# One of the last weight transfers of an attention and spectral-mixing kernel, issued as 16 pieces of 8 partitions

## The chip, the cores and the metric

The kernel runs on one core of a Trainium2 chip. The metric is the device time of one execution in microseconds (us). A run's time is a little longer than the span of its profile, which runs from the first to the last recorded instruction.

## The reference

The input is q, k and v of 8 batches, 8 heads, 576 positions and 64 channels, two stacks of 64 weight matrices of 512x512 (w_r and w_i), and one 512x512 matrix w_ch, all fp32. A sliding-window causal attention (window 64) comes first; its output, 8 x 576 x 512, goes through a mixing in the frequency domain.

```
scores = where(0 <= pos_q - pos_k < 64, q k^T / 8, -1e9)
x = softmax(scores) v                     # as [8, 576, 512]
X = rfft(x, axis=1)                       # the first 64 modes are kept
Yr = Xr w_r - Xi w_i                      # one 512x512 matrix per mode
Yi = Xr w_i + Xi w_r
y = irfft(Y, n=576)
u = x + y
out = u + max(u w_ch, 0)
```

The two weight stacks hold 2 x 64 x 512 x 512 x 4 B = 134 MB, and each weight is used once.

## The kernel before

**Stages.** Attention comes first, batch by batch, with the forward transform done as matmuls against tables of sines and cosines (`trigF`). Then, for each group of four modes, matmuls at line 175 multiply the transformed rows (`XQ`) by the weights. A tail transforms back, multiplies by `w_ch` and writes the output. Work is issued in the order in which it is written (a manual schedule); each engine has its own queue and works it off in order.

**The weights.** `wlist` is the order in which weights are loaded: 32 steps (a group of four modes and one half `hb` of the 512 input channels), each with w_r and then w_i (`ri` = 0 and 1), each of these as two loads of two modes. Two of these loads (of steps 3 and 31) are cut into two loads of one mode, so there are 130 loads, counted here from 0 by `nload`. A load reads fp32 from DRAM and writes bf16 to SBUF into a tile of 128 partitions x 2 modes x 2 rows x 512; 512 KB are written. All loads are issued on the queue of POOL (GpSimd), at line 156. The last group in this order is 13: step 30 is its first half, step 31 its second.

**Where loads go.** Two rings of tiles, `ringA` with 7 and `ringB` with 10, and some lent places hold the weights. From step 20 on (load 81 and later) only `ringA` is used. `load_weights` issues the next load when the ring's oldest tile is in `spent`, which `mode_half` fills after its matmuls are written down. So a load late in the kernel waits, on POOL, for the matmuls that used the load seven places ahead of it.

**The last nine loads** are 121 and 122 (w_r of step 30), 123 and 124 (w_i of step 30), 125 and 126 (w_r of step 31), 127 (w_i of step 31, two modes), and 128 and 129 (one mode each, 256 KB). `mode_half` for step 30 with `ri` = 0 uses loads 121 and 122, and its matmuls come on PE before those of all later loads. Between the calls of `mode_half`, `advance` puts other work on PE (lines 591 and 660).

**After the last load** PE multiplies, turns and transforms back; POOL has no DMA left and adds two tensors at line 731 in some of the output tiles. SP issues most of the output.

Of the kernel before, what the change touches and what calls it, by code (L numbers as in the profile page):

```python
# [17 lines left out]
NRA = 7  # L18
NRB = 10
WARM = 8  # L20
NEG = -1.0e30
MAGIC = 12582912.0
PSAFE = 3.14159
# [3 lines left out]
def kernel(  # L27
# [10 lines left out]
    nc = tc.nc  # L38
# [10 lines left out]
    HALF = DM // 2  # L49
    NJ = 2  # L50
# [51 lines left out]
    wlist = []  # L102
# [27 lines left out]
    nload = 0  # L130
# [5 lines left out]
    def load_weights(n):  # L136
        nonlocal nload
        while n > 0 and nload < len(wlist):
            at, ps, hb, ri = wlist[nload]
            if nload in lent:  # L140
                w = lent[nload]
            else:
                open_to = "a" if at >= 2 * EARLY else "aby" if at < EARLY + 2 else "ab"
                h = min(open_to, key=lambda h: held[h][0] if len(held[h]) == room[h] else -1)
                if len(held[h]) == room[h]:
                    if held[h][0] not in spent:
                        return
                    held[h].pop(0)
                held[h].append(nload)
                if h == "y":  # L150
                    w = lentY[0]
                    lentY.append(lentY.pop(0))
                else:
                    w = {"a": ringA, "b": ringB}[h].tile([128, 2, NJ, DM], BF16, name="wi" if ri else "wr", tag="wt")
            src = moe_w_i if ri else moe_w_r
            nc.gpsimd.dma_start(  # L156
                out=w[:, 0:len(ps)], in_=src[ps[0]:ps[-1] + 1, HALF * hb:HALF * hb + HALF, :].rearrange("g (p j) e -> p g j e", j=NJ))
            for i, p in enumerate(ps):
                wtiles[p, hb, ri] = w[:, i]
            nload += 1  # L160
            n -= len(ps)
# [26 lines left out]
    with tc.manual_schedule():  # L188
# [165 lines left out]
        warm = ps_m.tile([128, DM], FP32, name="warm", tag="misc")  # L354
        for _ in range(WARM):
            nc.tensor.matmul(out=warm, lhsT=idle[:, 0:128], rhs=idle, start=True, stop=True)
# [7 lines left out]
        at = scratch[:, 3 * NTF * NM:3 * NTF * NM + NTF]  # L364
# [8 lines left out]
        for nm in ("k", "q", "v"):  # L373
            load(1, nm)
        LEAD = 4
        load_weights(LEAD)
        nc.gpsimd.iota(Kb, pattern=[[64, NBLK]], base=0, channel_multiplier=0,
                       allow_small_or_imprecise_dtypes=True)
# [25 lines left out]
        prvm, curm = mask_t[:, 0, 0, 0:64], mask_t[:, 0, 0, 64:128]  # L404
        ve.tensor_scalar(out=curm, in0=Kf, scalar1=Mcol, scalar2=NEG, op0=ALU.is_gt, op1=ALU.mult)
        ve.tensor_scalar(out=prvm, in0=Kf, scalar1=Mcol, scalar2=NEG, op0=ALU.is_le, op1=ALU.mult)
        ve.tensor_copy(out=mask_t[:, 0, 1, :], in_=mask_t[:, 0, 0, :])
        ve.tensor_copy(out=mask_t[:, 0, 2:4, :], in_=mask_t[:, 0, 0:2, :])
        ve.tensor_copy(out=mask_t[:, 1], in_=mask_t[:, 0])
        ve.memset(mask_t[:, 1, 0:4:2, 0:64], NEG)  # L410

# [40 lines left out]
        def early_step(it):  # L452
            nonlocal step
            grp = step
            psm = ps_m.tile([128, DM], FP32, name="psm", tag="misc")
            for ri in range(2):
                mode_half(psm, grp, 0, ri, True, True)
                load_weights(due(it) - loaded())
            nc.scalar.copy(out=Yacc[grp], in_=psm)
            step += 1  # L460
# [4 lines left out]
        for it in range(-3, NU + 3):  # L465
# [23 lines left out]
            g = starts.get(it + 2)  # L489
# [3 lines left out]
            g = starts.get(it + 1)  # L493
            if g is not None and g + 2 < NG:
                load(g + 2, "v")
            if it >= 0:
                for f in trig[0:2]:
                    f()
                del trig[0:2]
            load_weights(due(it) - loaded())  # L500
        do_dft(NG - 1)
        while step < EARLY:
# [183 lines left out]
        pu, us, ps = {}, {}, {}  # L686
# [184 lines left out]
```

## Time and profile before

| | us |
|---|---|
| median of 3 runs | 441.37 (441.29 to 441.67) |
| the profiled execution | 441.02 |
| its span | 439.2 |
| PE busy | 350.0 (80%) |
| DVE busy | 219.9 (50%) |
| ACT busy | 173.7 (40%) |
| POOL busy | 143.4 (33%) |
| packets of the queue that POOL issues, share of 16 DMA engines | 98.6% |

A line of a timeline gives start, duration, engine, line, operation, out<-in and count; in square brackets stands the idle time of the engine just before it and what ended it. A line of the chain of waits gives start, duration and what the time went to. POOL's `DMA_DIRECT2D` is the issue of a transfer; the transfer lands later, and the profile gives the time from issue to landing by line. 15.9 us is the median for the w_i loads.

### The profile page before, as it was taken

What the parts mean: (1) busy time and instruction counts of PE and PEld (TensorE: products, weight loads), DVE (VectorE), ACT (ScalarE), POOL (GpSimd) and SP (SyncE); (2) the same over time, 40 slices, a digit from 0 to 9 for tenths busy, and PEclk for the clock granted to TensorE, in tenths of its full rate; (3) what the DMA queues carried; (4) which work ended last, traced back from release to release, by engine and by line L of the source; (5) the groups of instructions that cost most, each with busy time, mean ns of one, the idle gap of its engine ahead of it and who ended that gap; (6) DMA issues with size and microseconds to landing.
All of it is one profiled execution on the core that took longest, in us unless ns stands there. A gap on an engine that the chain in (4) does not pass through costs nothing.

```text
span 439.2 us, 10995 instructions
## 1 busy us (share of the span) xinstructions
PE 350.0 (80%) x4728; PEld 219.5 (50%) x4728; DVE 219.9 (50%) x447; ACT 173.7 (40%) x307; POOL 143.4 (33%) x211
## 2 busy tenths in 40 slices
PE   6999999998999997986336565766778766799994
PEld 3666767676767664662113223334454433453552
DVE  8588787876776763775014111212223122345773
ACT  5666667575667663533002101111122121124662
POOL 9333323323233233223232232122232222301773
PEclk9999999999999996988559556788889689899999
DMA  8999999999999999999999999999999999992887
GB/s 205 211 211 211 212 210 211 211 211 211 212 211 212 212 210 211 211 212 211 211 258 211 211 211 211 211 211 211 212 211 211 211 211 211 212 177 67 271 305 263
DMA packets 47873, 93.45 MB, mean 213 GB/s; under 512 B 3536, under 2 KB 3664, under 8 KB 47824
## 3 DMA queue, kind: packets, MB, share of 16 engines
q0 software_dynamic: 42000, 81.73, 98.6%
q1 hardware_dynamic: 5600, 10.62, 7.2%
q8 instruction: 37, 0.61, 0.5%
q10 hardware_dynamic: 224, 0.39, 0.3%
q14 instruction: 12, 0.10, 0.1%
HBM read 163.58 MB, written 9.44 MB: 394 GB/s over the span
## 4 chain that ended last, share of the span: by engine, by line
DMA 47%; PE 41%; issue 5%; ACT 3%; DVE 3%; POOL 1%; DVEq 0%; POOLq 0%
DMA wi<-in_moe_w_i_dram 24%; DMA wr<-in_moe_w_r_dram 11%; DMA rawk<-in_k_dram 7%; PE tr L222 6%; DMA wch<-in_moe_w_ch_dram 4%; PE s L269 4%; PE pt L289 4%; PE s L261 4%; PE s L281 3%; PE psm L175 3%; PE vb L234 3%; PE o L309 2%; PE psz L591 1%; PE psm L697 1%; PE pst L723 1%
## 5 line engine op out<-in xcount | busy, mean ns | idle before, releaser
L591 PE MATMUL psz<-wch,tr 128*128 128x512 f32 x176 | 67.2, 517 | 10.9 <-DMA wch<-in_moe_w_ch_dram 10.9
L156 POOL DMA_DIRECT2D wi<-in_moe_w_i_dram x62 | 43.9, 709 | 95.7 <-PE psm L175 49.2
L682 DVE CAST xw<-psz 128x512 fp32r<-128x512 f32 x36 | 24.9, 691 | 91.4 <-PE psz L591 90.9
L156 POOL DMA_DIRECT2D wr<-in_moe_w_r_dram x53 | 37.9, 714 | 87.9 <-PE psm L175 38.0
L175 PEld LDWEIGHTS <-XQ 128*32 128x32 bf16 x512 | 24.0, 165 | 81.0 <-issue 73.6
L273 DVE TENSOR_REDUCE mx<-s 128x4 fp32r<-128x512 f32 x72 | 49.5, 687 | 26.3 <-PE s L269 26.0
L568 ACT CAST tr<-ptx 128x512 fp32r<-128x512 bf16 x36 | 21.1, 587 | 103.8 <-PE ptx L584 103.8
L175 PE MATMUL psm<-wi,XQ 128*32 128x512 bf16 x244 | 34.0, 466 | 30.6 <-DMA wi<-in_moe_w_i_dram 30.6
L591 PEld LDWEIGHTS psz<-wch,tr 128*128 128x128 f32 x176 | 40.1, 252 | 17.4 <-issue 11.2
L175 PE MATMUL psm<-wr,XQ 128*32 128x512 bf16 x212 | 29.8, 485 | 22.0 <-DMA wr<-in_moe_w_r_dram 21.3
L283 ACT ACTIVATE p<-s 128x512 bf16<-128x512 f32 x72 | 39.8, 604 | 13.0 <-PE s L281 13.0
L226 ACT COPY kT<-tr 128x576 bf16<-128x576 bf16 x32 | 23.2, 724 | 24.4 <-PE tr L222 24.4
L731 POOL TENSOR_TENSOR ut<-ut,XQ 128x512 f32<-128x512 f32 x16 | 20.5, 1284 | 28.1 <-ACT XQ L730 27.5
L292 DVE COPY pts<-pt 128x1024 bf16<-128x1024 bf16 (+1 forms) x40 | 25.2, 629 | 8.3 <-PE pt L289 7.0
L269 PE MATMUL s<-kT,qT 64*64 64x128 bf16 (+1 forms) x576 | 29.2, 221 | 0.0
L261 PE MATMUL s<-mask_t,ident_bf 128*128 128x512 bf16 x72 | 28.4, 395 | 0.9 <-ACT p L283 0.8
L226 ACT COPY qT<-tr 128x576 bf16<-128x576 bf16 x32 | 23.3, 729 | 10.7 <-PE tr L222 10.7
L269 PEld LDWEIGHTS <-qT 64*64 64x64 bf16 x576 | 17.8, 107 | 18.0 <-issue 17.5
L281 PE MATMUL s<-mx,ident_r 128*128 128x512 f32 x72 | 26.4, 438 | 0.0
L289 PE MATMUL pt<-ident_bf,p 128*128 128x128 bf16 x288 | 23.8, 223 | 1.5 <-issue 1.3
L226 ACT COPY vT<-tr 128x576 bf16<-128x576 bf16 x32 | 23.3, 728 | 4.0 <-PE tr L222 3.9
L321 DVE TENSOR_TENSOR x_sb<-o,r 128x512 bf16<-128x512 f32 x32 | 22.1, 691 | 1.1
(182 smaller groups left out, 567.2 us busy)
## 6 DMA issues: line engine op xcount, KB each, us to landing
wi<-in_moe_w_i_dram POOLq DMA_DIRECT2D x60, 512.0 KB, 15.9
wr<-in_moe_w_r_dram POOLq DMA_DIRECT2D x53, 512.0 KB, 16.3
out_dram<-ut SPq DMA_DIRECT2D x31, 256.0 KB, 2.4
rawv<-in_v_dram POOLq DMA_DIRECT2D x16, 288.0 KB, 14.4
rawk<-in_k_dram POOLq DMA_DIRECT2D x15, 288.0 KB, 15.1
rawq<-in_q_dram POOLq DMA_DIRECT2D x15, 288.0 KB, 14.1
Ypair<-in_moe_w_r_dram POOLq DMA_DIRECT2D x5, 512.0 KB, 14.9
x_sb<-in_moe_w_r_dram POOLq DMA_DIRECT2D x4, 512.0 KB, 15.2
```

The source lines that it names most:

```text
L156: nc.gpsimd.dma_start(out=w[:, 0:len(ps)], in_=src[ps[0]:ps[-1] + 1, HALF * hb:HALF * hb + HALF, :].rearrange("g (p j) e -> p g j e", j=NJ))
L175: nc.tensor.matmul(out=psm[32 * g:32 * g + 32, :], lhsT=XQ[hb].rearrange("k s b m -> k (s b) m")[:, (3 * j + 1 - ri) * B:(3 * j + 5 - ri) ...
L222: nc.tensor.transpose(out=pt[ro, j, :], in_=raw[ro, TH * half + j, :], identity=ident_bf[ro, ro])
L226: nc.scalar.copy(out=to, in_=pt.rearrange("p j n -> p n j"))
L261: nc.tensor.matmul(out=s, lhsT=ident_bf, rhs=mask_t[:, mk], start=True, stop=True)
L269: nc.tensor.matmul(out=s[ro, t, lo:128], lhsT=lq, rhs=kT[ro, 64 * n - 64 + lo:64 * n + 64], start=False, stop=True, skip_group_check=True)
L273: nc.vector.tensor_reduce(out=mx, in_=s, axis=AX.X, op=ALU.max, negate=True)
L281: nc.tensor.matmul(out=s, lhsT=ident_r, rhs=mx.unsqueeze(2).to_broadcast([128, 4, 128]), start=False, stop=True, skip_group_check=True)
L283: nc.scalar.activation(out=p[:, 4 * c2:4 * c2 + 4, :], in_=s, func=ACT_F.Exp, scale=EX_SCALE)
L289: nc.tensor.transpose(out=pt[:, t, :], in_=st[u]["p"][:, t, :], identity=ident_bf)
L292: nc.vector.tensor_copy(out=ps[:, 0:nt, :], in_=pt[:, 0:nt, :])
L591: nc.tensor.matmul(out=pz, lhsT=tr[:, c, :], rhs=wch[:, c, :], start=(c == 0), stop=(c == NDCH - 1))
```

## The change

A load whose number is 9 before the end of the list (130 - 9 = 121, the first w_r load of step 30) is issued by a loop of 16 DMAs, each of 8 partitions, in place of one DMA of 128 partitions. The destination tile, the bytes and the place in the order are the same, and every other load goes through the same loop once.

```diff
+NSPLIT = 9
...
-            src = moe_w_i if ri else moe_w_r
-            nc.gpsimd.dma_start(
-                out=w[:, 0:len(ps)], in_=src[ps[0]:ps[-1] + 1, HALF * hb:HALF * hb + HALF, :].rearrange("g (p j) e -> p g j e", j=NJ))
+            src = (moe_w_i if ri else moe_w_r)[ps[0]:ps[-1] + 1, HALF * hb:HALF * hb + HALF, :]
+            src = src.rearrange("g (p j) e -> p g j e", j=NJ)
+            n8 = 8 if nload == len(wlist) - NSPLIT else 128
+            for at in range(0, 128, n8):
+                nc.gpsimd.dma_start(out=w[at:at + n8, 0:len(ps)], in_=src[at:at + n8])
```

## The prediction

> **What bounds the kernel now.** I read the page's DMA rows first, then POOL's timeline (early and late), then the end of the chain of waits, then PE's timeline around the load that is cut.
>
> ```profile
> GB/s 205 211 211 211 212 210 211 211 211 211 212 211 212 212 210 211 211 212 211 211 258 211 211 211 211 211 211 211 212 211 211 211 211 211 212 177 67 271 305 263
> ...
> q0 software_dynamic: 42000, 81.73, 98.6%
> ```
>
> The flow of weights is flat at 211 GB/s up to slice 35, and the DMA queue behind POOL is all of it. A load of 512 KB (524,288 B) takes 2.48 us at that rate. As long as something is queued this flow sets the time; a gap in it is lost.
>
> ```profile
> 9.50 0.74 POOL L156 DMA_DIRECT2D wi<-in_moe_w_i_dram  x1
> 10.23 0.57 POOL L209 DMA_DIRECT2D rawk<-in_k_dram  x1
> 10.78 0.56 POOL L209 DMA_DIRECT2D rawq<-in_q_dram  x1
> 11.32 0.73 POOL L156 DMA_DIRECT2D wi<-in_moe_w_i_dram  x1
> 12.49 0.55 POOL L209 DMA_DIRECT2D rawv<-in_v_dram  x1 [0.45 <-PE tr L222]
> 13.03 0.72 POOL L156 DMA_DIRECT2D wr<-in_moe_w_r_dram  x1
> 18.10 0.55 POOL L209 DMA_DIRECT2D rawk<-in_k_dram  x1 [4.35 <-DMA Ypair<-in_moe_w_r_dram]
> 18.64 0.55 POOL L209 DMA_DIRECT2D rawq<-in_q_dram  x1
> 20.68 0.71 POOL L156 DMA_DIRECT2D wr<-in_moe_w_r_dram  x1 [1.49 <-DMA wi<-in_moe_w_i_dram]
> 22.33 0.55 POOL L209 DMA_DIRECT2D rawv<-in_v_dram  x1 [0.95 <-PE vb L234]
> 23.51 0.70 POOL L156 DMA_DIRECT2D wi<-in_moe_w_i_dram  x1 [0.63 <-DMA rawq<-in_q_dram]
> ```
>
> This is the row that decides the case, and it lies far from the edit. The issue at 20.68 waited for the landing of a w_i load. Count back eight issues: the w_i load at 9.50. The issue at 23.51 waited for a rawq load; eight back stands rawq at 10.78. The trace's records of these issues name eight semaphores (104 to 111), taken in turn through all 177 issues of POOL. So an issue waits until the issue eight before it has landed: POOL has at most eight transfers under way, whatever their size.
>
> ```profile
> 363.04 0.71 POOL L156 DMA_DIRECT2D wi<-in_moe_w_i_dram  x1 [3.59 <-PE psm L175]
> 363.75 0.72 POOL L156 DMA_DIRECT2D wr<-in_moe_w_r_dram  x1
> 367.97 0.71 POOL L156 DMA_DIRECT2D wr<-in_moe_w_r_dram  x1 [3.50 <-PE psm L175]
> 368.68 0.72 POOL L156 DMA_DIRECT2D wi<-in_moe_w_i_dram  x1
> ...
> 382.94 1.10 POOL L156 DMA_DIRECT2D wi<-in_moe_w_i_dram  x2 [3.52 <-PE psm L175]
> ```
>
> These are loads 120, 121 (to be cut), 122, 123, and 128 with 129. Here PE's use of the tile seven loads back is what POOL waits for; the eighth transfer back has long landed. The two issues at 363 land after 14.1 and 15.9 us (minimum and maximum of their row), load 120 at 377.1 and load 121 at 379.6: some six loads lie in the queue.
>
> ```profile
> 377.93 14.12 DMA wr<-in_moe_w_r_dram
> 392.09 0.67 PE psm L175 x5
> ...
> 397.40 0.59 PE psm L175 x2
> ```
>
> ```profile
> 382.15 0.71 PE L175 MATMUL psm<-wr,XQ 128*32 128x512 bf16 x6 [2.03 <-DMA wr<-in_moe_w_r_dram]
> ```
>
> The chain goes from the issue of load 126 to its landing and into the last matmuls; PE resumes on load 122 at 382.15 after 2.03 us idle for it. The tail to the end hangs on these landings.
>
> **The change, step by step.** It removes one issue of 0.72 us on POOL and adds 16. The bytes stay.
>
> *Price of one piece.* No row has 16 rows of 2 KB (8 partitions x 2 modes). At line 156, 256 rows take 0.714 us and the 128 rows of loads 128 and 129 take 0.553 (0.548 and 0.558). That is 1.26 ns a row, so 16 rows come to 0.553 - 112 x 0.00126 = 0.41. Bounds: the shortest rows, 0.528 for 128 rows, give 0.37 by the same line, and I go down to 0.35; above, the full load's 0.71. I take 0.41.
>
> *Pieces 0 to 6* (16 pieces, from 0). Piece 0 waits for the transfer eight back, load 113, landed long ago; pieces 1 to 6 for loads 114 to 119. These land 2.48 us apart, so POOL now goes at the pace of landings. Their bytes (7/16 of 2.48 = 1.1 us) lie in the queue before load 120 has ended, and cost nothing.
>
> *Piece 7* waits for the transfer just ahead of the cut load, load 120: 377.1. In the early rows a freed issue starts 0.29 us after the last increment of the semaphore (landed 20.39, issued 20.68; 23.22 and 23.51). So piece 7 starts at 377.4, with only 1.1 us of bytes queued, half spent or more.
>
> *Pieces 7 to 15* follow one another: 9 x 0.41 = 3.7 us, to 381.1. Pieces 8 to 14 wait for pieces 0 to 6, landed by about 378.5; piece 15 waits for piece 7, issued 8 x 0.41 = 3.3 us before it, and isn't held if a piece lands within that time; by the price below it does (4.9 - 2.48, plus 0.16 of movement: 2.6). Queued behind all this on POOL are loads 122 to 129, and nothing else until 404.41 (line 731). Load 122 is thus issued at 381.1, not at 367.97.
>
> *Load 122 into an empty queue.* Every weight load of the trace finds a full queue, so I bound. Above: the first load of all, 288 KB, lands after 6.1 us; less 1.40 us of movement that leaves 4.7, in competition with SP's two loads of q and k. Below: SP's stores of 256 KB land after 2.4 us, of which 1.0 is movement at 263 GB/s: 1.4. With 2.48 of movement the load takes 3.9 to 7.2; I take 4.9, nearer to SP's rows, as theirs is the uncrowded queue, plus POOL's longer issue. It lands at 381.1 + 4.9 = 386.0; before, at 367.97 + 14.13 = 382.1. The loss is **3.9 us**. The Trainium skill ("DMA: Bandwidth & Descriptors", section "Anatomy of one DMA") puts the fixed part of a POOL transfer at about 2.0 us; with 2.48 of movement that would make 4.5, and the loss 3.5. No row here has it.
>
> *What passes on.* Loads 123 to 127 follow 0.71 us apart, faster than they move; their tiles are free by then (load 127 needs load 120's matmuls, done near 378). Loads 128 and 129 need the matmuls of 121 and 122, some two us after 386.0, with five loads or 12.4 us still queued. So the flow is whole again from 122 on, and every later landing is late by the same 3.9. On PE, from 382.15 to the wait at 392.09 there is hardly a gap, in an order that is fixed, so that nothing can be drawn forward into the longer wait. The first matmul on the cut load waits on up to eight semaphores for one; at 17 ns a semaphore row that is 0.14 us, under the wait for load 122, and would cost that 0.14 without it. A longer idle PE might also be clocked down: after the 2 us waits at 372.20 and 382.15 the four matmuls of line 591 took 2.06 us, later ones 1.17. They pay this already, so I add 0, at most 0.9.
>
> Sum: 441.02 of the profiled execution + 3.9 = 444.9; against the median, 441.37 + 3.9 = **445.3**.
>
> Ends: 0.35 a piece and 3.9 for load 122 give 377.4 + 3.15 + 3.9 = 384.45, +2.35. A piece at 0.71 alone gives +6.6; load 122 at 7.2 alone gives, with piece 15 then held by piece 7, about +7.8.
>
> **Rivals.**
>
> *Not held: no change.* If pieces don't wait eight back, POOL is busy 16 x 0.41 = 6.6 us from 363.75 to 370.4, and load 122 is issued 2.4 us late into a queue that lasts to 379.6; load 124 at 373.09 is on time again. 441.4. Against it: the early rows, where the waits stand.
>
> *The other side: trailing engines relieved.* A load's semaphore rises in 16 steps. For load 121 eight come from 374.0 to 376.1 and eight from 378.5 to 379.6; for load 129 from 391.5 to 393.5 and from 395.9 to 397.2. Eight engines trail and set each landing. If every piece's data went to the leading eight, these would end 2.48 later, at 396.0, and the trailing eight 2.48 sooner: 1.2 us gained, 440.2. It decides only if piece 7 isn't held, since held, the trailing engines sit idle for longer than the 2.48 they save. The Trainium skill (same page, "Why a DMA increments its semaphore by 16 and not by 1") says that 8 partitions usually go to 8 engines, taken by a cursor that moves on, which spreads them evenly and gives nothing; it has an exception with one partition per engine, which would use the same eight each time. The trace doesn't name the engines.
>
> *A floor per transfer.* If each small piece occupied the engines as long as a lone store's fixed 1.4 us, pieces 7 to 15 would end at 377.4 + 9 x 1.4 = 390.0, and load 122 would land 12.8 us late: 454. Against it: loads 128 and 129, half as long, land within 2.7 us together (394.5 to 397.2), where one whole load takes 2.48. The Trainium skill (same page, section "Bandwidth") has transfers under 64 KB as dominated by their descriptors, 0.95 us for 64 KB; 16 in a row would be 15 us by an estimate from it.
>
> **How the numbers follow.** Forecast 0.87, not held 0.06, relieved 0.04, floor 0.03. A difference of 0.2% (0.9 us) is what this measurement can tell. So slower 0.90, same 0.06, faster 0.04. The range is the forecast's own, +2.1 to +7.8 over the median: 443.5 to 449.2; both prices at their upper ends together are left out, as are the rivals.
>
> **What would show it.** Right: on POOL's timeline the pieces come first at the pace of landings; then one waits for a w_i load (load 120) to about 377.4; nine issues of about 0.4 us follow; load 122 is issued near 381; the DMA share dips between 378 and 384; PE waits some 6 us for load 122; the chain holds POOL's issues. Wrong: load 122 issued before 372, or no dip, or a piece far from 0.41.

## The result

| | before | after |
|---|---|---|
| median, us | 441.33 (441.27 to 441.67, 4 runs) | 448.46 (447.64 to 448.81, 4 runs) |
| profiled execution, us | 441.02 | 448.37 |
| its span, us | 439.2 | 446.6 |

The change makes the kernel slower: ratio 1.0157 (95% interval 1.014 to 1.0175), +7.1 us. The forecast was +3.9, the range +2.1 to +7.8. Side and mechanism came out as forecast, the size nearly twice as large.

Two rows of the page of the changed kernel (the flow by slices, and the queue that POOL issues on):

```profile
GB/s 206 209 213 209 211 211 211 210 211 212 210 211 211 211 212 210 211 212 211 234 234 211 211 211 212 211 211 211 211 212 211 211 211 131 127 211 62 268 288 281
...
q0 software_dynamic: 42496, 81.74, 97.4%
```

Counted from 0, the flow is near 211 GB/s in nearly every slice up to 32 before and after (around slice 20 both hold more). The two slices around the cut load, 33 and 34, have 131 and 127, where before they had 211 and 212. A slice is 11.2 us, so (80 + 84) / 211 x 11.2 = 8.7 us of flow are missing there. Half of the increments of a load's semaphore came some 4.5 us ahead of the other half, and this lead was given up (below); over all 16 that is 2.2 of the 8.7, and 6.5 are left, by this estimate.

POOL's timeline there; load 120 is the first line, and the pieces have the line `wr` until the one marked x10, which holds pieces 7 to 15 and load 122:

```profile
363.20 0.72 POOL L160 DMA_DIRECT2D wi<-in_moe_w_i_dram  x1 [3.56 <-PE psm L178]
363.91 1.76 POOL L160 DMA_DIRECT2D wr<-in_moe_w_r_dram  x3
367.61 0.55 POOL L160 DMA_DIRECT2D wr<-in_moe_w_r_dram  x1 [1.93 <-DMA wi<-in_moe_w_i_dram]
370.13 0.55 POOL L160 DMA_DIRECT2D wr<-in_moe_w_r_dram  x1 [1.97 <-DMA wr<-in_moe_w_r_dram]
372.62 0.55 POOL L160 DMA_DIRECT2D wr<-in_moe_w_r_dram  x1 [1.93 <-DMA wr<-in_moe_w_r_dram]
375.06 0.55 POOL L160 DMA_DIRECT2D wr<-in_moe_w_r_dram  x1 [1.89 <-DMA wi<-in_moe_w_i_dram]
377.60 6.10 POOL L160 DMA_DIRECT2D wr<-in_moe_w_r_dram  x10 [1.99 <-DMA wi<-in_moe_w_i_dram]
383.70 1.46 POOL L160 DMA_DIRECT2D wi<-in_moe_w_i_dram  x2
```

From piece 3 on (367.61) the waits for a landing show in brackets, and the issues come 2.5 us apart: 367.61, 370.13, 372.62, 375.06, 377.60. That is the pace of whole loads, imposed on pieces of a sixteenth. After the last such wait ten issues follow without a pause.

The same stretch as busy time by engine (us, PE, PEld, DVE, ACT and POOL with counts, then granted clock, DMA share, GB/s), three microseconds a line:

```profile
377.00:380.00 3.00, 3.00 (x19) 1.46 (x17) 1.72 (x3) 0.56 (x1) 2.40 (x4) 0.76 0.22 32
380.00:383.00 3.00, 0.16 (x1) 0.00 (x0) 1.03 (x2) 0.59 (x1) 3.00 (x7) 1.00 0.41 52
383.00:386.00 3.00, 0.44 (x2) 0.18 (x3) 0.00 (x0) 0.00 (x0) 3.00 (x5) 0.87 0.72 93
```

The flow is down to 32, 52 and 93 GB/s. From 380 on POOL is the only engine that is busy throughout, and PE all but stands still. PE's timeline shows for whom it waits, loads 121 and 122:

```profile
384.91 0.44 PE L178 MATMUL psm<-wr,XQ 128*32 128x512 bf16 x2 [4.75 <-DMA wr<-in_moe_w_r_dram]
388.38 1.10 PE L178 MATMUL psm<-wr,XQ 128*32 128x512 bf16 x6 [3.02 <-DMA wr<-in_moe_w_r_dram]
```

Before, PE resumed on load 122 at 382.15, so it is 6.2 us late here. In the chain of waits (start, duration, what) POOL itself now stands between two landings, where before one issue was enough:

```profile
363.20 14.12 DMA wi<-in_moe_w_i_dram
377.32 0.28 issue
377.60 4.20 POOL wr L160 x7
...
385.14 1.42 POOL wr L160 x2
386.56 15.79 DMA wi<-in_moe_w_i_dram
402.39 0.66 PE psm L178 x4
```

Load 120 lands at 377.32, piece 7 starts 0.28 us later, and everything up to the last loads hangs on POOL's row of issues.

### The profile page after: what moved, and what is told of

Its sections match the earlier page's. It is cut to its first block, busy times and chain, and to the rows that moved or that the text cites. A ratio compares the mean times of both kernels' runs of the same rounds, so it can differ in the third digit from the quotient of the medians.

```text
span 446.6 us, 11009 instructions
## 1 busy us (share of the span) xinstructions
PE 344.3 (77%) x4728; PEld 213.5 (48%) x4728; DVE 219.5 (49%) x447; ACT 173.8 (39%) x307; POOL 152.2 (34%) x226
## 4 chain that ended last, share of the span: by engine, by line
DMA 49%; PE 35%; issue 6%; ACT 3%; DVE 3%; POOL 2%; DVEq 0%; POOLq 0%
DMA wr<-in_moe_w_r_dram 32%; DMA rawk<-in_k_dram 7%; DMA wi<-in_moe_w_i_dram 7%; PE tr L225 5%; PE s L272 4%; PE psm L178 3%; DMA rawq<-in_q_dram 3%; PE s L264 3%; PE pt L292 3%; PE vb L237 3%; PE s L284 3%; PE o L312 2%; POOL wr L160 2%; PE psm L700 1%; PE psz L700 1%
## 5 line engine op out<-in xcount | busy, mean ns | idle before, releaser
L160 POOL DMA_DIRECT2D wr<-in_moe_w_r_dram x68 | 46.5, 684 | 87.5 <-DMA wr<-in_moe_w_r_dram 31.0
L594 PE MATMUL psz<-wch,tr 128*128 128x512 f32 x176 | 63.0, 490 | 10.9 <-DMA wch<-in_moe_w_ch_dram 10.9
L178 PE MATMUL psm<-wr,XQ 128*32 128x512 bf16 x212 | 30.8, 502 | 33.8 <-DMA wr<-in_moe_w_r_dram 33.2
L594 PEld LDWEIGHTS psz<-wch,tr 128*128 128x128 f32 x176 | 37.0, 234 | 16.9 <-issue 11.1
## 6 DMA issues: line engine op xcount, KB each, us to landing
rawk<-in_k_dram POOLq DMA_DIRECT2D x15, 288.0 KB, 15.1
Ypair<-in_moe_w_r_dram POOLq DMA_DIRECT2D x5, 512.0 KB, 15.1
x_sb<-in_moe_w_r_dram POOLq DMA_DIRECT2D x4, 512.0 KB, 15.1
```

The source lines that it names most:

```text
L160: nc.gpsimd.dma_start(out=w[at:at + n8, 0:len(ps)], in_=src[at:at + n8])
L178: nc.tensor.matmul(out=psm[32 * g:32 * g + 32, :], lhsT=XQ[hb].rearrange("k s b m -> k (s b) m")[:, (3 * j + 1 - ri) * B:(3 * j + 5 - ri) ...
L594: nc.tensor.matmul(out=pz, lhsT=tr[:, c, :], rhs=wch[:, c, :], start=(c == 0), stop=(c == NDCH - 1))
```

## The experiments

"Held" is the theory of the prediction: POOL has at most eight transfers under way, so sixteen small ones empty the DMA queue. Its main rival is a cost for each added issue, 7.1 us / 15 = 0.48 us. All kernels differ from the changed kernel only in the place shown. Before was timed beside them: 441.44.

### Fewer pieces

```diff
-            n8 = 8 if nload == len(wlist) - NSPLIT else 128
+            n8 = 32 if nload == len(wlist) - NSPLIT else 128
```

> Load 121 cut into 4 pieces of 32 partitions. Held theory (at most eight of POOL's transfers under way): the pieces wait for loads 113 to 116, load 122 for load 117, which lands at 369.7; four pieces and four whole loads are still queued (12.4 us of movement) when load 122 is issued, so no gap: within 0.5 us of before, 441.4. Rival, a cost for each added issue (7.1 us / 15 = 0.48 us): 3 added issues, 442.8.

Measured 441.61, ratio 1.0004 (0.9995 to 1.0013). POOL's timeline, with pieces 0 to 2, piece 3 and load 122:

```profile
363.84 1.72 POOL L160 DMA_DIRECT2D wr<-in_moe_w_r_dram  x3
367.51 0.54 POOL L160 DMA_DIRECT2D wr<-in_moe_w_r_dram  x1 [1.95 <-DMA wi<-in_moe_w_i_dram]
370.31 0.72 POOL L160 DMA_DIRECT2D wr<-in_moe_w_r_dram  x1 [2.26 <-DMA wr<-in_moe_w_r_dram]
```

The wait for the landing eight back is there too, and load 122 is issued 2.3 us late (370.31 for 367.97). Three whole loads and the four pieces are still queued, 9.9 us of movement (the expectation counts one load too many), and the last piece lands at 380.04. So nothing comes of the delay: load 122 landed 11.94 us after its issue at 382.25, for 382.11 before.

```diff
-            n8 = 8 if nload == len(wlist) - NSPLIT else 128
+            n8 = 16 if nload == len(wlist) - NSPLIT else 128
```

> Load 121 cut into 8 pieces of 16 partitions. Held theory: piece 7 waits for load 120 (377.1), load 122 follows at 378.0 and its data comes 2.9 us later (5.37 to landing in the changed kernel, less 2.48 of movement), 380.9; the pieces' bytes last to 379.6, so a gap of 1.2 us: 442.6, at most 0.8 more where the leading engines' lead is lost. Rival, 0.48 us for each added issue: 7 added, 444.7.

Measured 443.66, ratio 1.0053 (1.0036 to 1.0069): +2.2, above the held theory's first figure and 0.3 over its upper end of 443.4, so the sum was short here; the rival's 444.7 is 1.0 off. The step lies between four pieces and eight. Piece 7 with load 122 (x2), after the wait for load 120:

```profile
375.11 0.50 POOL L160 DMA_DIRECT2D wr<-in_moe_w_r_dram  x1 [1.95 <-DMA wi<-in_moe_w_i_dram]
377.66 1.26 POOL L160 DMA_DIRECT2D wr<-in_moe_w_r_dram  x2 [2.05 <-DMA wi<-in_moe_w_i_dram]
```

Load 122 is issued at 378.2 and lands after 6.07 us at 384.26, 2.2 us late; 15 of its 16 increments were there within 5.6 us, and the last came 0.45 later. The expectation had taken 5.37 us for this landing; the 0.7 more is what it was short by.

```diff
-            n8 = 8 if nload == len(wlist) - NSPLIT else 128
-            for at in range(0, 128, n8):
+            cuts = 8 * [8] + 4 * [16] if nload == len(wlist) - NSPLIT else [128]
+            at = 0
+            for n8 in cuts:
                 nc.gpsimd.dma_start(out=w[at:at + n8, 0:len(ps)], in_=src[at:at + n8])
+                at += n8
```

> Load 121 cut into 12 pieces, eight of 8 partitions and four of 16. Held theory: five pieces (7 to 11) stand between the landing of load 120 and the issue of load 122, against one with 8 pieces (+2.2 us) and nine with 16 (+7.1 us): 0.61 us for each piece from piece 7 on, so +2.2 + 4 x 0.61 = +4.7, 446.1. Rival, the eighth piece alone brings the loss and the others hide behind it: 443.7.

Measured 446.03, ratio 1.0105 (1.009 to 1.012): +4.6. The row after the wait for load 120 holds the five pieces and load 122:

```profile
377.66 3.33 POOL L161 DMA_DIRECT2D wr<-in_moe_w_r_dram  x6 [1.98 <-DMA wi<-in_moe_w_i_dram]
```

So 4 pieces cost nothing that can be told, 8 cost 2.2, 12 cost 4.6, 16 cost 7.1. Beyond the eighth piece each costs about 0.6 us, the length of an issue; no cost for each issue from the first fits that.

### As many issues, but larger

```diff
-            n8 = 8 if nload == len(wlist) - NSPLIT else 128
+            n8 = 64 if 0 <= len(wlist) - NSPLIT - nload < 16 else 128
```

> Loads 106 to 121 are each issued as two pieces of 64 partitions: 16 added issues, one more than in the changed kernel, but each piece moves 1.24 us. Held theory: eight pieces under way are 9.9 us of movement, more than the 2.9 us from an issue to the first data, and POOL's price of about 0.6 us is below 1.24, so no gap: within 0.5 us of before, 441.4. Rival, 0.48 us for each added issue wherever it stands: 449.1.

Measured 441.68, ratio 1.0007 (0.9998 to 1.0016). Sixteen added issues, no loss that can be told.

```profile
364.37 0.59 POOL L160 DMA_DIRECT2D wi<-in_moe_w_i_dram  x1 [0.91 <-DMA wi<-in_moe_w_i_dram]
365.42 0.59 POOL L160 DMA_DIRECT2D wi<-in_moe_w_i_dram  x1 [0.47 <-DMA wi<-in_moe_w_i_dram]
366.89 0.59 POOL L160 DMA_DIRECT2D wi<-in_moe_w_i_dram  x1 [0.88 <-DMA wi<-in_moe_w_i_dram]
```

Here too each issue waits for the landing eight back. The waits are harmless, because eight halves are 9.9 us of movement.

### POOL busy, no pieces

```diff
+    dummy = consts.tile([128, 512], BF16, name="dummy")
...
-            n8 = 8 if nload == len(wlist) - NSPLIT else 128
-            for at in range(0, 128, n8):
-                nc.gpsimd.dma_start(out=w[at:at + n8, 0:len(ps)], in_=src[at:at + n8])
+            nc.gpsimd.dma_start(out=w[:, 0:len(ps)], in_=src)
+            if nload == len(wlist) - NSPLIT:
+                for _ in range(10):
+                    nc.gpsimd.memset(dummy, 0.0)
```

> Load 121 stays whole; behind its issue POOL clears a scratch tile ten times (some 5 to 6 us of POOL time, as much as the pieces 7 to 15 take), which no one reads. Held theory: load 122 is issued some 2 us late into a queue that lasts to 379.6, no gap: 441.4 within 0.5 us. Rival, POOL's time in front of load 122 is itself the cost: 447 or so.

Measured 441.46, ratio 1.0003 (0.9993 to 1.0012).

```profile
365.62 6.25 POOL L162 MEMSET dummy<- 128x512 bf16 x10
371.81 0.72 POOL L159 DMA_DIRECT2D wr<-in_moe_w_r_dram  x1
```

Load 122 went out 3.8 us later than before (some 2 were expected), behind 6.25 us of other work, and the time stayed. So POOL's time is hidden as long as the queue is full. In the changed kernel 5.36 us of issues delay everything behind them, because they come after load 120's landing, when the queue runs empty.

### Another shape, another place, twice

```diff
-            n8 = 8 if nload == len(wlist) - NSPLIT else 128
-            for at in range(0, 128, n8):
-                nc.gpsimd.dma_start(out=w[at:at + n8, 0:len(ps)], in_=src[at:at + n8])
+            if nload == len(wlist) - NSPLIT:
+                for at in range(0, 128, 32):
+                    for i in range(len(ps)):
+                        for j in range(NJ):
+                            nc.gpsimd.dma_start(out=w[at:at + 32, i, j], in_=src[at:at + 32, i, j])
+            else:
+                nc.gpsimd.dma_start(out=w[:, 0:len(ps)], in_=src)
```

> Load 121 as 16 pieces of 32 partitions x one row of one mode, again 32 KB each, in packets of 1 KB instead of 2 KB. Held theory: the number of issues and their bytes decide, so the same as the changed kernel within 0.7 us, 448.4. Rival, that pieces of 8 partitions are slow for the DMA engines (only some of the 16 take part): most of the loss goes, below 445.

Measured 447.36, ratio 1.0136 (1.0121 to 1.0151): +5.9, 0.3 us below the interval given, and far from the rival's. The 1.1 us that it saves against the changed kernel are mostly POOL's:

```profile
377.81 4.50 POOL L162 DMA_DIRECT2D wr<-in_moe_w_r_dram  x9 [2.00 <-DMA wi<-in_moe_w_i_dram]
382.30 0.74 POOL L164 DMA_DIRECT2D wr<-in_moe_w_r_dram  x1
```

Nine pieces take 4.50 us, for 5.36 (377.60 to 382.96) with pieces of 8 partitions: 0.86 of the 1.1.

```diff
-            n8 = 8 if nload == len(wlist) - NSPLIT else 128
+            n8 = 8 if nload == 100 else 128
```

> The 16 pieces of 8 partitions on load 100 instead of load 121, some 52 us earlier. Held theory: a gap in the flow of weights is lost wherever it stands, +6.2 to +7.1: 447.6 to 448.5. Rival, a gap that early is made up by the 30 loads that follow: 441.4.

Measured 448.63, ratio 1.0162 (1.0145 to 1.0179): 0.13 us over the figures given, and the same loss as at the end. Nothing later makes up for a gap.

```profile
325.42 4.93 POOL L160 DMA_DIRECT2D wi<-in_moe_w_i_dram  x9 [2.23 <-DMA wi<-in_moe_w_i_dram]
```

The nine pieces took 0.4 us less here. Against before, the loads from 102 to 115 land 6.7 to 6.9 us late, and from load 116 on 7.4 to 7.9 ("What passes on", below, has the step).

```diff
-            n8 = 8 if nload == len(wlist) - NSPLIT else 128
+            n8 = 8 if nload in (len(wlist) - NSPLIT, len(wlist) - NSPLIT - 10) else 128
```

> Loads 111 and 121 are both cut into 16 pieces of 8 partitions. Held theory: two gaps, each lost in full, +12.4 to +14.2: 453.8 to 455.6. Rival, the second gap is cheaper or free since the first already made POOL late: 448.5 to 450.

Measured 455.95, ratio 1.0333 (1.0316 to 1.035): +14.5, twice the loss, 0.35 above the upper figure.

In all ten traces POOL's issues (177 to 207 of them) never have more than eight transfers under way, and none starts less than 0.27 us after the landing of the one eight before it. No run changed the number eight itself.

## Why the prediction was right, and where it was short

Each term against the profile after:

| term | forecast, us | measured, us | difference |
|---|---|---|---|
| start of piece 7 | 377.4 | 377.60 | +0.2 |
| pieces 7 to 15, 9 issues | 3.7 | 5.36 | +1.7 |
| load 122 from issue to landing | 4.9 | 5.37 | +0.5 |
| landing of load 122 to that of load 129 | 15.1, as before | 15.90 | +0.8 |
| from there to the end of the span | 42.0, as before | 42.3 | +0.3 |

The differences are 3.5 us, and with the forecast's 3.9 they give the 7.4 by which the span grew.

The side and the path were right, and so the range held; the forecast itself was little more than half of what came. Of the signs that it named, the pace, the wait for load 120, the dip and POOL in the chain came. Load 122 went out at 382.96 and not near 381, and a piece took 0.55 to 0.81 and not 0.41, which it had put among its signs of being wrong. PE's wait of "some 6 us for load 122" came in two parts, 4.75 for load 121 and 3.02 for load 122, as the last piece of 121 landed only at 384.77. The ends of the range were added up loosely: the lower one comes to +2.35 and was given as +2.1, and the upper one leaves out the 0.29 us between landing and issue, with which it is +8.1.

**The wait eight back** was right in place and time: the pieces came at the pace of the landings, the hold ended on a w_i load at 377.32, and pieces 8 to 15 weren't held again. A piece from 377.6 on lands 2.2 to 2.9 us after its issue, below the 3.3 that would have held piece 15. The row that told all this stood some 340 us ahead of the edit.

**The price of a piece** is the step that failed in size: "16 rows come to 0.41". I drew a line through the prices of 256 rows (0.714) and 128 rows (0.553) and went on to 16. There is no such line below 128 rows. Pieces of 16 rows take 0.55, of 32 rows 0.50 (with 8 pieces) and 0.50 (4.50 / 9, the other shape), of 64 rows 0.54, of 128 rows 0.59 in the halves. The issue of a transfer of 16 to 64 rows has a floor of about half a microsecond here. Of the 1.7 us by which the term was short, 9 x 0.14 = 1.3 are this price, and 0.4 are two pieces that took longer still (last section). The 4.50 us of the other shape and the time it saved show that this price passes into the time.

**The empty queue** was right within 0.5: 5.37 for 512 KB, between 3.9 and 7.2. What is not movement is 5.37 - 2.48 = 2.9 us. With 8 and 12 pieces, with the other shape and with load 100 cut, the first whole load behind the pieces took 5.57 to 6.22, so 3.1 to 3.7. The rule of the Trainium skill ("DMA: Bandwidth & Descriptors", section "Anatomy of one DMA") of about 2.0 us was 0.9 short for this load; pieces 7 to 15, at 2.2 to 2.9 with 0.16 of movement, are nearer to it.

**What passes on** was short by 0.8. Before, eight of a load's 16 increments led by some 4.5 us, so a delay of one of those eight alone did not delay a landing. In the changed kernel the pause lets the trailing eight catch up: the 16 increments of load 122 come within 0.55 us of each other, where those of load 121 spread over 5.6 us before. After that a delay of any one of them is a delay of the landing. Load 127's increments came from 400.2 to 401.0 and one at 402.35; a packet of 16 KB of the instruction queue, 0.97 us long, starts at 400.3. The same shows twice more. With load 100 cut, such a packet of 0.95 us starts at 372.74, and the last increment of load 116 comes at 375.02, 1.1 us after the fifteenth; from there on the loads are that much later. With two loads cut, one of 0.94 us starts at 373.05, and again load 116's last increment comes 1.1 us after the fifteenth (375.14 and 374.01). That the packet lay on the engine of that increment is argued from the times; the trace doesn't name engines. The other kernels of the experiments have 14.9 to 15.6 for this term.

The longer idle time of PE cost no more clock: the four matmuls of line 594 behind the wait took 1.82 us, where before they took 2.06 (line 591).

**The rivals.** "Not held" falls with the waits on POOL's timeline. "Trailing engines relieved" falls with the hold; besides, in the full queue both the leading and the trailing increments move on by about 0.18 us with each piece, so neither half got more than the other. "A floor per transfer" on the DMA engines falls too: pieces 7 to 15 land 0.60 us apart on average ((384.77 - 379.95) / 8), the pace of their issues, and 1.4 would have been needed.

## What to carry to other kernels

Count what a queue can have under way in transfers, and turn it into time: here eight of 2.48 us are 20 us of cover, eight of 0.155 us are 1.2, less than the 2.9 that load 122 took beside its movement. Cutting one load into four cost nothing, into eight 2.2 us; sixteen added pieces that each move longer (1.24 us) than their own issue takes (0.59) cost nothing either. Five to seven pieces weren't tried; by the theory seven would lose something already, as load 122 would then itself wait for load 120. Price a small transfer with the floor of the nearest rows, not with the line through them, and look for the limit in another stage of the same kernel, where it binds already.

## What was not expected of the hardware

Two of the nine pieces took longer than 0.55 us: in POOL's rows starting at 378.70 (two pieces) and 380.05 (three), one piece each took 0.81 and 0.73. DVE's casts of line 660 lie within exactly these two:

```profile
378.70 1.35 POOL L160 DMA_DIRECT2D wr<-in_moe_w_r_dram  x2
380.05 1.82 POOL L160 DMA_DIRECT2D wr<-in_moe_w_r_dram  x3
```

```profile
379.54 0.42 DVE L660 CAST tr<-Yall 128x512 fp32r<-128x512 bf16 x1
...
380.81 0.42 DVE L660 CAST tr<-Yall 128x512 fp32r<-128x512 bf16 x1
```

1.35 less 0.55 is 0.80, and 1.82 less twice 0.55 is 0.72. The Trainium skill ("SBUF — State Buffer", the "DVE blocks DMA" trap) says that POOL is locked out of a port it shares with DVE, and can't write a DMA's descriptors, while DVE runs an instruction in a two-port mode. The trace doesn't show the mode of these casts. The other traces have four more pieces with such a cast wholly inside their issue: one with 12 pieces, one of the other shape, two with two loads cut. All six took 0.04 to 0.26 us longer than their neighbours, and each ended 0.10 us after its cast. Against it, the issue of a whole load that held such a cast (371.98 with the halves) took its usual 0.72 us. So a piece seems to wait for the cast; it wasn't tried by itself.
